# Softmax maxima over partitions: from a GpSimd all-reduce to VectorE's 32x32 transposes, with the subtraction on GpSimd

## The chip, the cores and the metric

One core of a Trainium2 chip. The time is device microseconds of one execution of the whole program. Five engines run their own queues in order: TensorE (PE), VectorE (DVE), ScalarE (ACT), GpSimd (POOL) and SyncE (SP, which issues most DMAs). Each engine does its instructions in the order of the program and waits on semaphores for what it needs.

## The reference

An attention block and a gated feed-forward block on the same input, mixed by a gate; all in float32. S = 2048 tokens, D = 448, 16 heads of 28, F = 1792.

```
g = sigmoid((x * gate_w).sum(-1))
q, k, v = heads of x @ wqkv
a = softmax(q k^T * 28**-0.5) v @ wo
b = (relu(x @ W_gate) * (x @ W_up)) @ W_down
out = g * a + (1 - g) * b
```

The softmax needs, for each query, a number near the maximum of its 2048 scores, to be subtracted before the exponential.

## The kernel before

**Stages.** Up to about 122 us x is projected to q, k and v (lines 292 to 510). Then come 32 *visits* of attention, two for each head: an even visit takes the first 1024 keys of a head, an odd one the other 1024. From about 1063 us the rest of the feed-forward block and the output projection run.

**Two ways to a maximum.** Scores are kept transposed, keys on partitions and queries along the free dimension. For 1536 of the 2048 queries of a head (three blocks of 512) the maximum is found ahead of time: `smax` (L161) computes the scores a second time with queries on partitions (products *sm*, L169), DVE reduces each of them with L171, and after the last one `smax_end` (L178) turns the maxima into two more rows of Q, so that the products *s* of the visit (L264, in `score`) come with the maximum already subtracted, and ACT applies the exponential straight from PSUM (L268). For the fourth block (`TQ = 1`) the raw scores are copied out by ACT with the sign turned (L270) into *quads*, tiles of 128 x 4 x 512. `block_min` takes the minimum over their chunks on DVE (L220, L222, into `r2`, then L228 into `rm`, L230 or L232 for the sign and the two halves); `all_max` reduces `rm` over the partitions on GpSimd (L238); `take_max` adds it to each of the two quads on DVE (L247); `take_exp` applies the exponential on ACT (L254). `rescale` brings the first half of a head to the maximum of the second (L592, L595, L596).

**The order.** It is written out by hand as strings, one per visit (L45 to L53), read letter by letter by the loop at L667: `s` a pair of score products, `m` an sm product with its L171, `x` one matmul of the feed-forward block (L554, filling PE's time), `b` a step of `block_min`, `A` is `all_max`, `g` is `take_max`, `e` is `take_exp`, `P` and `Q` the two halves of the product with V (`pv`, L608, after which L616 on DVE adds the two halves of a head), `w` the splitting of feed-forward weights (L109), `c` and `f` the two parts of `rescale`, `n` is `smax_end`. Visit 0 uses FIRST, visits 3, 8, 11 and 20 WIDE (called *long* here, four units of the feed-forward block), the other visits up to 28 LONG (*short*, three units), and 29 to 31 LATE, where no sm products are left. The minima of a visit are taken ahead of its `A`, at the end of the visit before.

**PSUM.** Every s and sm product takes one of three buffers of 128 x 1024 (`ps_w`, L92): two of tag `mx` and one of tag `w`, every third product the latter. An s is emptied by ACT, an sm by DVE's L171.

Of the kernel before, what the change touches and what calls it, by code (L numbers as in the profile page):

```python
# [1 line left out]

# [17 lines left out]
P = 128  # L20
# [9 lines left out]
TB = 512  # L30
# [36 lines left out]
def gated_mix_kernel(ctx, tc, x, wq, wo, wgu, wd, out):  # L67
    nc = tc.nc
# [30 lines left out]
    def ps_x(name):  # L99
        return psum.tile([P, TB], F32, tag="x", bufs=2, name=name)  # L100
# [89 lines left out]
    AT, QUAD, slots = {}, {}, iter(range(10 ** 6))  # L190
# [15 lines left out]

    stream = [p for v in range(2 * H) for p in visit(v)]
    todo_max, todo_sub, todo_exp, todo_all = [], [], [], []
    RM, R2, left = {}, {}, {}

    def block_min():

        if not todo_max:
# [13 lines left out]
        RM[v, b] = r  # L227
        nc.vector.tensor_tensor(r, r2[:, 0], r2[:, 1], op=OP.min)  # L228
        if v % 2:
            nc.vector.scalar_tensor_tensor(r, r, -1.0, RM[v - 1, b], op0=OP.mult, op1=OP.max)  # L230
        else:
            nc.vector.tensor_scalar(r, r, -1.0, None, op0=OP.mult)  # L232
        q = NK // 8 * (v % 2)
        todo_all.append((v, b, [(v, j, q), (v, j, q + 1)]))

    def all_max():
        v, b, quads = todo_all.pop(0)
        nc.gpsimd.partition_all_reduce(RM[v, b], RM[v, b], P, bass_isa.ReduceOp.max)  # L238
        todo_sub.extend((v, b, q) for q in quads)

    def take_max(way):
        v, b, q = todo_sub.pop(0)
        m = RM[v, b].unsqueeze(1).to_broadcast([P, 4, TB])
        if way == "d":
            nc.gpsimd.dma_start(QUAD[q], m, accum_op=OP.add)
        else:
            nc.vector.tensor_tensor(QUAD[q], QUAD[q], m, op=OP.add)  # L247
# [44 lines left out]
    with tc.tile_pool(name="qkv", bufs=1) as pa:  # L292
# [189 lines left out]
        m, first, ahead = 0, 9, NM[0] + NM[1] // 2  # L482
# [38 lines left out]
    att = stk.enter_context(tc.tile_pool(name="att", bufs=1))  # L521
# [395 lines left out]
```

## Time and profile before

| | us |
|---|---|
| median of 2 runs (1269.86 to 1271.8) | 1270.83 |
| the profiled execution | 1270.4 |
| its span | 1268.6 |
| PE busy | 1238.7 |
| DVE busy | 973.5 |
| ACT busy | 765.0 |
| POOL busy | 159.2 |

Engines overlap, so the busy times don't add up to the span. A busy PE is not a PE at its peak. The granted TensorE clock was 0.997 of full speed over the span. What counts is which engine's wait ends last at each place; the rows are read in the prediction. In rows of the timeline the columns are start, length, engine, line, operation, output<-input, shapes, count, and in brackets the idle time ahead with what ended it. In rows of groups: line, engine, operation, shapes, count, then busy us and mean ns of one, then idle us ahead. In rows of waits: who waited for whom, us in total, times, the longest.

### The profile page before, as it was taken

Reading aid. Unit: us, or ns where it says so; the run is one execution under the profiler, and the core shown is the slowest. Engines: PE = TensorE matmul, PEld = TensorE weight load, DVE = VectorE, ACT = ScalarE, POOL = GpSimd, SP = SyncE. Lnnn points to the kernel's source line nnn. Section 1 sums busy time; section 2 is a strip of 40 time slices with the busy share of each in tenths; the row PEclk is TensorE's granted clock in tenths of the full one; section 3 lists DMA queues with packets and bytes.
Section 4 is the critical chain, followed back from the end, with each engine's and each line's share of the span. In section 5 each row is a group of like instructions: output and inputs, shape, how many; then the busy total and the mean of one; then the engine's idle time right before and its main releaser. Section 6 shows DMA issues by size and latency. Waiting matters only on the chain.

```text
span 1268.6 us, 16622 instructions
## 1 busy us (share of the span) xinstructions
PE 1238.7 (98%) x6431; PEld 865.4 (68%) x6431; DVE 973.5 (77%) x985; ACT 765.0 (60%) x894; POOL 159.2 (13%) x146
## 2 busy tenths in 40 slices
PE   9999899999999999999999999999999799999998
PEld 6888556656566666666666666666666466899998
DVE  6466799999999989899998899898998262563342
ACT  5312667868676777777776767767766684222121
POOL 4222100000010000000001000000001011541020
PEclk9999999999999999999999999999999899999999
DMA  8946544352527252524545251424442226744432
GB/s 299 313 184 237 159 144 123 121 171 75 167 70 243 103 150 75 151 68 119 146 148 141 78 150 55 133 95 112 120 153 91 76 91 212 230 142 153 138 112 79
DMA packets 64299, 178.48 MB, mean 141 GB/s; under 512 B 13746, under 2 KB 20594, under 8 KB 59570
## 3 DMA queue, kind: packets, MB, share of 16 engines
q1 hardware_dynamic: 57484, 151.13, 39.5%
q0 software_dynamic: 6304, 25.82, 5.3%
q8 instruction: 51, 0.84, 0.3%
q10 hardware_dynamic: 432, 0.46, 0.1%
q14 instruction: 28, 0.23, 0.1%
HBM read 118.58 MB, written 58.87 MB: 140 GB/s over the span
## 4 chain that ended last, share of the span: by engine, by line
PE 86%; DVE 6%; ACT 3%; DMA 3%; issue 1%; POOL 1%; SPq 0%; ACTq 0%; DVEq 0%; POOLq 0%
PE gu L554 19%; PE s L264 18%; PE po L608 16%; PE sm L169 13%; PE acc L816 10%; PE qk L385 5%; PE wo L775 3%; PE v L403 3%; DVE mx L171 2%; ACT P L268 1%; DVE wg L109 1%; DVE P L247 1%; ACT P L254 1%; DVE r L222 1%; DMA wg<-ws_d 1%
## 5 line engine op out<-in xcount | busy, mean ns | idle before, releaser
L171 DVE TENSOR_REDUCE mx<-sm 128x1 f32<-128x1024 f32 x384 | 459.2, 1218 | 68.1 <-PE sm L169 66.7
L554 PE MATMUL gu<-X,wg 128*128 128x512 f32 x1232 | 366.8, 395 | 2.2 <-DMA wg<-ws_d 2.2
L268 ACT ACTIVATE P<-s 128x1024 f32<-128x1024 f32 x306 | 295.1, 1025 | 94.3 <-PE s L264 92.6
L264 PE MATMUL s<-Q,K 128*128 128x512 f32 x1024 | 318.3, 403 | 13.7 <-DMA Q<-mh 6.4
L554 PEld LDWEIGHTS gu<-X,wg 128*128 128x128 f32 x1232 | 231.3, 188 | 60.5 <-DMA wg<-ws_d 2.6
L169 PE MATMUL sm<-K,Q 128*128 128x512 f32 x768 | 242.5, 398 | 6.7 <-DVE mx L171 4.3
L264 PEld LDWEIGHTS s<-Q,K 128*128 128x128 f32 x1024 | 184.8, 189 | 85.8 <-issue 18.5
L608 PE MATMUL po<-P,V 128*32 128x512 f32 x1640 | 227.6, 596 | 0.8 <-ACT P L254 0.8
L169 PEld LDWEIGHTS sm<-K,Q 128*128 128x128 f32 x768 | 134.1, 188 | 55.7 <-DVE mx L171 13.2
L238 POOL PARTITION_ALL_REDUCE rm<-rm x32 | 66.5, 2079 | 832.2 <-DVE rm L230 415.3
L608 PEld LDWEIGHTS po<-P,V 128*32 128x32 f32 x1640 | 61.0, 110 | 119.4 <-issue 117.0
L816 PE MATMUL acc<-WD,hh 128*128 128x448 f32 x672 | 138.5, 365 | 0.0
L270 ACT ACTIVATE P<-s 128x1024 f32<-128x1024 f32 x104 | 105.9, 1026 | 52.9 <-PE s L264 50.3
L816 PEld LDWEIGHTS acc<-WD,hh 128*128 128x128 f32 x672 | 126.2, 188 | 10.4
L247 DVE TENSOR_TENSOR P<-P,rm 128x2048 f32<-128x2048 f32 x52 | 117.5, 2268 | 5.6 <-POOL rm L238 5.6
L608 PE MATMUL po<-V 128*32 128x512 f32 x408 | 116.4, 597 | 0.0
L103 ACT ACTIVATE hh<-hr 128x512 fp32r<-128x512 f32 x56 | 35.3, 631 | 118.7 <-PE acc L816 113.3
L254 ACT ACTIVATE P<-P 128x2048 f32<-128x2048 f32 x52 | 99.5, 1913 | 2.3 <-DVE P L247 2.1
L109 DVE TENSOR_TENSOR hh<-hr,hh 128x512 fp32r<-128x512 f32 x56 | 49.1, 877 | 62.4 <-ACT hh L103 62.4
L268 ACT ACTIVATE V<-s 128x1024 f32<-128x1024 f32 x78 | 76.3, 1026 | 22.1 <-PE s L264 21.6
L385 PE MATMUL qk<-X,W 128*128 128x512 f32 x308 | 77.4, 397 | 0.4 <-DVE X L109 0.2
L567 DVE TENSOR_TENSOR h<-gu,rl 128x512 f32<-128x512 f32 x56 | 38.2, 681 | 42.9 <-ACT rl L564 21.7
(82 smaller groups left out, 858.1 us busy)
## 6 DMA issues: line engine op xcount, KB each, us to landing
wg<-ws_d SPq DMA_DIRECT2D x42, 896.0 KB
K<-qk_d SPq DMA_DIRECT2D x64, 224.0 KB
Q<-qk_d SPq DMA_DIRECT2D x64, 224.0 KB
h_d<-h SPq DMA_DIRECT2D x56, 256.0 KB
hr<-h_d SPq DMA_DIRECT2D x56, 256.0 KB
ws_d<-wg SPq DMA_DIRECT2D x14, 896.0 KB
qk_d<-st POOLq DMA_DIRECT2D x21, 512.0 KB, 3.3
wgr<-wgu SPq DMA_DIRECT2D x13, 512.0 KB
```

Source lines behind the costliest of these rows:

```text
L169: nc.tensor.matmul(ps[:, c, :], Q[h][:, u * P:(u + 1) * P], K[h % 3][:, k0:k0 + TB], start=True, stop=True)
L171: nc.vector.tensor_reduce(MX[h][:, 2 * u + half:2 * u + half + 1], ps, axis=AX.XY, op=OP.max)
L238: nc.gpsimd.partition_all_reduce(RM[v, b], RM[v, b], P, bass_isa.ReduceOp.max)
L247: nc.vector.tensor_tensor(QUAD[q], QUAD[q], m, op=OP.add)
L254: nc.scalar.activation(q, q, AF.Exp, scale=-SCALE)
L264: nc.tensor.matmul(ps[:, c], K[h % 3][:, k * P:(k + 1) * P], Q[h][:, j * TB:(j + 1) * TB], start=True, stop=True)
L268: nc.scalar.activation(dst, ps, AF.Exp, scale=SCALE)
L270: nc.scalar.activation(dst, ps, AF.Copy, scale=-1.0)
L385: nc.tensor.matmul(ps, W[:, a, c * P:(c + 1) * P], xf(tb, b), start=(n == 0), stop=(n == NT - 1))
L554: nc.tensor.matmul(ps, WS[i][:, s, a], xf(i // NF, b), start=(n == 0), stop=(n == NT - 1))
L608: nc.tensor.matmul(po[32 * j:32 * j + 32], V[:, h // 4 % 2, k, h % 4], AT.pop((v, k, j)), start=(k == k0), stop=(k == k0 + NK // 2 - 1))
L816: nc.tensor.matmul(ACC[i // NF][t][:, :D], HH[i][:, a, t * P:(t + 1) * P], WD[:, f, b], start=(f == 0 and n == 0), stop=(f == NF - 1 and n ...
```

## The change

The maximum over partitions leaves GpSimd. `all_max` now does on DVE: a transposing reduction of `r2` (each 32 x 32 block is transposed and reduced over what were its 32 partitions), three copies that bring the other three groups of 32 partitions to the first, a reduction over the four groups and both halves of `r2` (and, in an odd visit, over the result of the even one), three copies back to the other groups, and a transpose of the repeated result that gives a tile of 128 x 512 with the same row on every partition. `take_max` subtracts it from the quads on GpSimd, a quarter of a quad at a time. L228, L230, L232 and the all-reduce go, and both `g` stand right behind `A`. `rescale` subtracts 32 x 16 numbers and transposes them.

```
-FIRST = "mmbslmxusbssmsxbxsxmxxsmxxmmsxxsxsAxgbxsmsbxxxxmmxegmxxbxxPweQ"
+FIRST = "mmbslmxusbssmsxbxsxmxxsmxxmmsxxsxsAggxbxsmsbxxxxmmxemxxbxxPweQ"
-LONG = "AnsmsxxxxsxxssxgmxxxxsmsxxsxssgxmxsxxmsmxxxmsmxxxxscmxsxemxxxbxxsmxbmbPefwQ"
+LONG = "AggnsmsxxxxsxxssxmxxxxsmsxxsxssxmxsxxmsmxxxmsmxxxxscmxsxemxxxbxxsmxbmbPefwQ"
...
-        r, r2 = att.tile([P, TB], F32, name=f"rm_{v}_{b}", tag=f"rm{v % 2}{b}", bufs=1), R2[v, b]
-        nc.vector.tensor_tensor(r, r2[:, 0], r2[:, 1], op=OP.min)
-        if v % 2:
-            nc.vector.scalar_tensor_tensor(r, r, -1.0, RM[v - 1, b], op0=OP.mult, op1=OP.max)
-        else:
-            nc.vector.tensor_scalar(r, r, -1.0, None, op0=OP.mult)
...
     def all_max():
-        nc.gpsimd.partition_all_reduce(RM[v, b], RM[v, b], P, bass_isa.ReduceOp.max)
+        v, b, j, quads = todo_all.pop(0)
+        h, odd = v // 2, v % 2
+        if not odd:
+            MN[h, b] = att.tile([P, 10, 16], F32, name=f"mn_{h}_{b}", tag=f"mn{b}", bufs=1)
+        n, to = MN[h, b], 8 + odd
+        nc.vector.tensor_reduce(n[:, :2], R2.pop((v, b)).rearrange("p a (b r) -> p a b r", r=32), axis=AX.X, op=OP.min,
+                                apply_transpose=True)
+        for k in range(1, 4):
+            nc.vector.tensor_copy(n[:32, 2 * k:2 * k + 2], n[32 * k:32 * k + 32, :2])
+        nc.vector.tensor_reduce(n[:32, to], n[:32, :to].rearrange("p a b -> p b a"), axis=AX.X, op=OP.min)
+        for k in range(1, 4):
+            nc.vector.tensor_copy(n[32 * k:32 * k + 32, to], n[:32, to])
+        RM[v, b] = att.tile([P, TB], F32, name=f"rm_{v}_{b}", tag="rm", bufs=2)
+        nc.vector.transpose(RM[v, b], n[:, to].unsqueeze(2).to_broadcast([P, 16, 32]))
         todo_sub.extend((v, b, q) for q in quads)
...
-            nc.vector.tensor_tensor(QUAD[q], QUAD[q], m, op=OP.add)
+        for c in range(0, 4, 1):
+            nc.gpsimd.tensor_tensor(QUAD[q][:, c], QUAD[q][:, c], RM[v, b], op=OP.subtract)
...
-        nc.gpsimd.partition_all_reduce(warm_r, warm_r, P, bass_isa.ReduceOp.max)
...
-                nc.vector.tensor_tensor(RS[h][r], RM[v - 1, b][r], RM[v, b][r], op=OP.subtract)
+                w = MN[h, b]
+                nc.vector.tensor_tensor(MN[h, 0][r, 0], w[r, 9], w[r, 8], op=OP.subtract)
+            nc.vector.transpose(RS[h][rows], MN[h, 0][rows, 0].unsqueeze(2).to_broadcast([32 * n, 16, 32]))
```

WIDE and LATE change in the same way: `gg` right behind `A`, and no other `g`. The orders of PE, ACT and SP stay as they are; those of DVE and POOL move. Where lines shift, the rows of the changed program carry its own line numbers (L170 is the old L171, L265 the old L264).

**DVE at the start of visit 16** (a short even visit; `r_16` is the `r2` of that visit, `mn` and `rm` the small tile and the result, `sm` the first sm product of the visit). Before:

```order
508 L222 TENSOR_TENSOR r_16_0_4973<-r_16_0_4973,P_3_1_4959 128x1024
509 L228 TENSOR_TENSOR rm_0_4998<-r_16_0_4973 128x512
510 L232 TENSOR_SCALAR rm_0_4998<-rm_0_4998 128x512
511 L596 TENSOR_TENSOR os_4803<-os_4803,rs_4952 32x512
512 L616 TENSOR_TENSOR os_4803<-po_5001,os_4803 128x512
513 L171 TENSOR_REDUCE mx_4825<-sm_5047 128x1
514 L247 TENSOR_TENSOR P_3_0_4932<-P_3_0_4932,rm_0_4998 128x2048
```

Now:

```order
531 L221 TENSOR_TENSOR r_16_0_5178<-r_16_0_5178,P_3_1_5164 128x1024
532 L596 TENSOR_TENSOR os_4992<-os_4992,rs_5156 32x512
533 L616 TENSOR_TENSOR os_4992<-po_5203,os_4992 128x512
534 L234 TENSOR_REDUCE mn_0_5243<-r_16_0_5178 128x32
535 L237 COPY mn_0_5243<-mn_0_5243 32x32 x3
536 L238 TENSOR_REDUCE mn_0_5243<-mn_0_5243 32x16
537 L240 COPY mn_0_5243<-mn_0_5243 32x16 x3
538 L242 STREAM_TRANSPOSE rm_0_5252<-mn_0_5243 128x512
539 L170 TENSOR_REDUCE mx_5031<-sm_5267 128x1
```

What stood ahead of L616 (L228, L232) is gone, and nine steps stand between L616 and the first reduction of the visit's sm products.

**DVE in visit 11** (a long odd visit, where `A` stands behind the second `m`). Before:

```order
393 L171 TENSOR_REDUCE mx_3888<-sm_3889 128x1
394 L171 TENSOR_REDUCE mx_3888<-sm_3904 128x1
395 L171 TENSOR_REDUCE mx_3888<-sm_3914 128x1
396 L247 TENSOR_TENSOR P_3_2_3751<-P_3_2_3751,rm_0_3818 128x2048
397 L247 TENSOR_TENSOR P_3_3_3776<-P_3_3_3776,rm_0_3818 128x2048
```

Now:

```order
407 L170 TENSOR_REDUCE mx_4025<-sm_4041 128x1
408 L234 TENSOR_REDUCE mn_0_3746<-r_11_0_3930 128x32
409 L237 COPY mn_0_3746<-mn_0_3746 32x32 x3
410 L238 TENSOR_REDUCE mn_0_3746<-mn_0_3746 32x16
411 L240 COPY mn_0_3746<-mn_0_3746 32x16 x3
412 L242 STREAM_TRANSPOSE rm_0_4054<-mn_0_3746 128x512
413 L170 TENSOR_REDUCE mx_4025<-sm_4068 128x1
```

The chain stands between the second and the third reduction, and the two L247 behind them are gone.

**PE in visit 16**, from its fourth product (`s_0_2`) on; in brackets the engines whose semaphores a row waits for. Before:

```order
2044 L264 MATMUL s_0_2_5061<-Q_1182,K_104 128x512 [waits Activation_49]
2045 L264 MATMUL s_0_2_5061<-Q_1182,K_104 128x512
2046 L554 MATMUL gu_0_5055<-X_111,wg_4869 128x512
2047 L554 MATMUL gu_0_5055<-X_112,wg_4869 128x512
2048 L264 MATMUL s_2_0_5068<-Q_1182,K_104 128x512 [waits DVE_49]
2049 L264 MATMUL s_2_0_5068<-Q_1182,K_104 128x512
2050 L264 MATMUL s_3_0_5072<-Q_1182,K_104 128x512 [waits Activation_49]
2051 L264 MATMUL s_3_0_5072<-Q_1182,K_104 128x512
2052 L554 MATMUL gu_0_5055<-X_111,wg_4869 128x512
2053 L169 MATMUL sm_5078<-K_102,Q_105 128x512 [waits Activation_49]
```

Now:

```order
2040 L265 MATMUL s_0_2_5281<-Q_1179,K_104 128x512 [waits Activation_49]
2041 L265 MATMUL s_0_2_5281<-Q_1179,K_104 128x512
2042 L552 MATMUL gu_0_5275<-X_111,wg_5074 128x512
2043 L552 MATMUL gu_0_5275<-X_112,wg_5074 128x512
2044 L265 MATMUL s_2_0_5288<-Q_1179,K_104 128x512 [waits Activation_49]
2045 L265 MATMUL s_2_0_5288<-Q_1179,K_104 128x512
2046 L265 MATMUL s_3_0_5292<-Q_1179,K_104 128x512 x2
2047 L552 MATMUL gu_0_5275<-X_111,wg_5074 128x512
2048 L168 MATMUL sm_5297<-K_102,Q_105 128x512 [waits DVE_49]
2049 L168 MATMUL sm_5297<-K_102,Q_105 128x512
```

PE's order is the same, but the wait for DVE, that is for the buffer of the visit's first sm product, has moved from the fifth product of the visit to the seventh, and the fifth waits for ACT. The buffers of the two are handed out when the program is built, by its own estimate of which comes free first. So it is in visits 4, 10, 16, 22 and 28; in 6, 12, 18 and 24 the wait for DVE stands at the eighth product, with the sixth waiting for ACT; in 2, 14 and 26 it stays at the fifth. In the long visits 8, 11 and 20 the buffer of the third sm product stays with the eleventh product, and in 3 it moves to the fourteenth.

More of the change, by code (lines that the diff above doesn't have):

```diff
@@ L3 @@
 import concourse.bass as bass
-import concourse.bass_isa as bass_isa
 import concourse.tile as tile
@@ L43 @@
 NP = 10
-FIRST = "mmbslmxusbssmsxbxsxmxxsmxxmmsxxsxsAxgbxsmsbxxxxmmxegmxxbxxPweQ"
-LONG = "AnsmsxxxxsxxssxgmxxxxsmsxxsxssgxmxsxxmsmxxxmsmxxxxscmxsxemxxxbxxsmxbmbPefwQ"
-WIDE = "ssnsxxmxxxsxxxmxAsmxxsxsxxxssxxxsxxgsxgmxxxsxmsxemxcxxxxmsxmxxxxxbsmbxxsxxmxxxemmbfPwQ"
-LATE = "xssxbxxxbxsAxsgxxgxsxxxsxxxsxxxsxsexxsxxwxsxxxxxxsxxxxcxxxsxxxxxxfnesbssPQ"
+FIRST = "mmbslmxusbssmsxbxsxmxxsmxxmmsxxsxsAggxbxsmsbxxxxmmxemxxbxxPweQ"
+LONG = "AggnsmsxxxxsxxssxmxxxxsmsxxsxssxmxsxxmsmxxxmsmxxxxscmxsxemxxxbxxsmxbmbPefwQ"
+WIDE = "ssnsxxmxxxsxxxmxAggsmxxsxsxxxssxxxsxxsxmxxxsxmsxemxcxxxxmsxmxxxxxbsmbxxsxxmxxxemmbfPwQ"
+LATE = "xssxbxxxbxsAggxsxxxsxxxsxxxsxxxsxsexxsxxwxsxxxxxxsxxxxcxxxsxxxxxxfnesbssPQ"
 ROUNDS = [(FIRST, 2)] + [(WIDE, 4) if k in (2, 7, 10, 19) else (LONG, 3) for k in range(2 * H - 4)] + [(LATE, 4)] * 3
@@ L208, in gated_mix_kernel @@
     todo_max, todo_sub, todo_exp, todo_all = [], [], [], []
-    RM, R2, left = {}, {}, {}
+    RM, R2, MN, left = {}, {}, {}, {}
     def block_min():
@@ L242, in take_max @@
         v, b, q = todo_sub.pop(0)
[L243 to L247, printed above, removed]
+        for c in range(0, 4, 1):
+            nc.gpsimd.tensor_tensor(QUAD[q][:, c], QUAD[q][:, c], RM[v, b], op=OP.subtract)
         todo_exp.append(q)
@@ L427, in gated_mix_kernel @@
         nc.vector.memset(warm, 0.0)
-        warm_r = pa.tile([P, 16], F32, name="warm_r")
-        nc.vector.memset(warm_r, 0.0)
         ps = ps_x("warm_ps")
```

4 lines of the change are left out of this document (1 added, 3 removed).

## Prediction

> **What bounds the kernel now.** I read the page's busy line first, then busy time by stretch, then PE's waits.
>
> ```profile
> PE 1238.7 (98%) x6431; PEld 865.4 (68%) x6431; DVE 973.5 (77%) x985; ACT 765.0 (60%) x894; POOL 159.2 (13%) x146
> 747.00:971.00 224.00, 224.00 (x1222) 142.69 (x1221) 202.85 (x191) 161.17 (x170) 17.25 (x12) 1.00 0.38 111
> PE s L264 <- DVE mx L171: 5.9, 9, 1.8
> PE sm L169 <- DVE mx L171: 4.3, 4, 2.1
> ```
>
> PE sets the end: in eight visits of attention (the second row: length, then PE, PEld, DVE, ACT, POOL) it is busy for all of 224 us, while DVE works 91% of them. Only 30 us of the span are without PE, so no relief of another engine can bring more, and what DVE costs PE is 5.9 + 4.3 = 10.2 us, none of it in that stretch. So the question is not how much DVE work goes, but whether DVE is late somewhere that PE stands waiting. Such a place exists at the start of every visit: each product (s or sm) takes one of three PSUM buffers, and PE needs a buffer back about three products later. A visit's first sm is given back by its L171.
>
> **What goes and what comes, on DVE.**
>
> ```profile
> L228 DVE TENSOR_TENSOR rm<-r 128x512 f32<-128x512 f32 x32 | 22.2, 692 | 1.1
> L232 DVE TENSOR_SCALAR rm<-rm 128x512 f32<-128x512 f32 x16 | 6.8, 427 | 0.5
> L247 DVE TENSOR_TENSOR P<-P,rm 128x2048 f32<-128x2048 f32 x52 | 117.5, 2268 | 5.6 <-POOL rm L238 5.6
> L171 DVE TENSOR_REDUCE mx<-sm 128x1 f32<-128x1024 f32 x384 | 459.2, 1218 | 68.1 <-PE sm L169 66.7
> L515 DVE TENSOR_SCALAR e<-e 128x16 f32<-128x16 f32 x1 | 0.2, 174 | 1.3 <-ACT e L514 1.3
> L109 DVE TENSOR_TENSOR mh<-mr,mh 16x128 fp32r<-16x128 f32 x16 | 4.4, 278 | 17.4 <-ACT mh L185 17.4
> ```
>
> Gone per visit: L228 0.69, L232 0.43 or its odd twin L230 at about 0.69, two L247 of 2.27: 5.8 us. New is one unbroken chain of nine steps. Nothing in the trace transposes, so I price by size. The transposing reduction of 1024 elements like L171, 1.22; six copies of 16 or 32 elements like L515, 0.18 each, 1.08; the reduction of 128 or 144 elements like mh, 0.29; the transpose to 512 elements like L228, 0.69; eight gaps of 0.03 (below, L232 starts 0.73 after an L228 of 0.69). Together **3.52 us**. Bounds: if the copies overlap and cost about half, and the second reduction 0.18, 2.5 us; if both transposing steps run at half rate (1.05 and 0.53 more), 5.1 us. I take 3.52, since each step has a row of its own size. L592 becomes a small step and a transpose, 0.17 longer, every other visit. DVE is thus relieved of about 2.2 us a visit, but the chain stands in one piece at the start of a visit, where before only L228 and L232 stood, ahead of PE's P and Q products.
>
> [...]
>
> **Start of a short even visit (v=16).**
>
> ```profile
> 609.50 0.69 DVE L228 TENSOR_TENSOR rm<-r 128x512 f32<-128x512 f32 x1
> 610.23 0.43 DVE L232 TENSOR_SCALAR rm<-rm 128x512 f32<-128x512 f32 x1
> 611.47 0.73 PE L264 MATMUL s<-Q,K 128*128 128x512 f32 x2
> 611.61 0.69 DVE L616 TENSOR_TENSOR os<-po,os 128x512 f32<-128x512 f32 x1 [0.24 <-PE po L608]
> 612.70 1.22 DVE L171 TENSOR_REDUCE mx<-sm 128x1 f32<-128x1024 f32 x1 [0.40 <-PE sm L169]
> 614.63 2.86 ACT L268 ACTIVATE P<-s 128x1024 f32<-128x1024 f32 x3 [0.39 <-PE s L264]
> 614.83 1.09 PE L264 MATMUL s<-Q,K 128*128 128x512 f32 x4
> 615.98 0.63 PE L169 MATMUL sm<-K,Q 128*128 128x512 f32 x2
> ```
>
> L616 waits for the last P and Q product and ends at 612.30 whatever goes before it. The chain stands behind it: 612.3 to 615.85. The first L171, done at 613.92 now, ends at 617.05. PE's fifth product, which takes that buffer today, starts at 614.83: **2.2 us** lost where the order stays so (v=14, 26; also 2). In other visits the buffers are handed out anew, as the order with the change shows. In v=10, 16, 22, 28 (and 4) the seventh product takes it; its fifth waits for ACT to empty the fourth (615.66), and the seventh, 615.98 today, for 617.05: **1.07**. In v=12, 18, 24 (and 6) it is the eighth; the sixth waits for ACT to empty the fifth, about 616.6 instead of 615.3: **1.3**. Sum of the nine from v=10: 2 x 2.2 + 4 x 1.07 + 3 x 1.3 = 12.6 us.
>
> **Odd visits (v=15)** have L634 in L616's place, and it waits for no product.
>
> ```profile
> 582.03 0.69 DVE L634 TENSOR_TENSOR os<-os,rb 128x512 f32<-128x512 f32 x1
> 584.50 0.28 DVE L109 TENSOR_TENSOR mh<-mr,mh 16x128 fp32r<-16x128 f32 x1 [1.79 <-ACT mh L185]
> 584.71 1.21 DVE L171 TENSOR_REDUCE mx<-sm 128x1 f32<-128x1024 f32 x1
> 586.62 0.63 PE L264 MATMUL s<-Q,K 128*128 128x512 f32 x2
> ```
>
> Without L228 and L230, L634 moves up 1.4 to 580.65, the chain runs 581.4 to 584.95, and mh and L171 end at 586.4, just ahead of 586.62: 0. The 1.79 us that DVE waits here today hide it; with a chain of 5.1 they would not, and nine visits would lose 1.4 each.
>
> **Long visits (v=11)** have the chain between the second and third L171.
>
> ```profile
> 472.96 2.38 DVE L171 TENSOR_REDUCE mx<-sm 128x1 f32<-128x1024 f32 x2 [0.35 <-PE sm L169]
> 473.46 0.62 PE L169 MATMUL sm<-K,Q 128*128 128x512 f32 x2
> 476.24 1.08 PE L264 MATMUL s<-Q,K 128*128 128x512 f32 x4
> ```
>
> The second ends at 474.15, the chain at 477.65, the third at 478.87. Its buffer is wanted at 476.24: 2.6 each in v=8, 11, 20; in v=3, where a later product takes it, I put ACT's 1.3. Sum 9.1.
>
> **Early visits**, with weight splits (L109) ahead of the chain:
>
> ```profile
> 265.23 1.19 PE L264 MATMUL s<-Q,K 128*128 128x512 f32 x4 [1.75 <-DVE mx L171]
> 353.28 1.21 DVE L171 TENSOR_REDUCE mx<-sm 128x1 f32<-128x1024 f32 x1
> ```
>
> Here DVE is already what PE waits for. Less 1.2 (L228, L232) and plus 3.55, the first L171 ends 2.35 later: v=2 loses 2.3; v=4, whose wait moves to the seventh product, 1.2; v=6, to the eighth, 0.2. In v=5 and 7 the L171 of the second row has 0.2 to spare and comes 2.1 later: 1.9 each. Sum 7.5.
>
> **GpSimd.** Eight subtractions of 512 elements a visit.
>
> ```profile
> L112 POOL TENSOR_TENSOR WD<-wdr,WD 128x448 fp32r<-128x448 f32 x14 | 21.4, 1527 | 51.5 <-DMA wdr<-wd 27.7 <-DVE WD L106 23.7
> L112 POOL TENSOR_TENSOR on<-or,on 128x1024 fp32r<-128x1024 f32 x8 | 19.6, 2456 | 56.2 <-ACT on L103 56.2
> 633.60 1.91 ACT L254 ACTIVATE P<-P 128x2048 f32<-128x2048 f32 x1
> ```
>
> Between the two sizes lie 1.61 ns an element, so 1.63 us a quarter, 6.5 a quad, 13.0 a visit: in v=16 from 615.85 to 628.9, ahead of the second exp (L254) at 633.60, which PE's delay moves back by another microsecond; the first exp needs only the quad that is ready at 622.4. Cost 0, as long as a quarter stays under (634.7 - 615.85) / 8 = 2.35 us. Beyond that ACT would stand at the exp, and behind it in ACT's queue the emptying of PSUM buffers that PE wants. Queued behind the quarters on GpSimd is only the small memset of m (L175), needed at the end of the visit: 0. The warm-up all-reduce at the program's start and its memset go too; only GpSimd's own memsets stood behind them: 0.
>
> [...]
>
> ```profile
> 155.52 2.28 DVE L247 TENSOR_TENSOR P<-P,rm 128x2048 f32<-128x2048 f32 x1
> 163.39 2.28 DVE L247 TENSOR_TENSOR P<-P,rm 128x2048 f32<-128x2048 f32 x1
> 165.70 1.91 ACT L254 ACTIVATE P<-P 128x2048 f32<-128x2048 f32 x1 [1.90 <-DVE P L247]
> 167.66 0.62 PE L608 MATMUL po<-P,V 128*32 128x512 f32 x1 [0.77 <-ACT P L254]
> 170.11 3.46 DVE L109 TENSOR_TENSOR wg<-wgr,wg 128x384 fp32r<-128x384 f32 x6
> 1085.33 0.39 DVE L106 CAST WD<-wdr 128x448 fp32r<-128x448 f32 x1
> 1093.99 4.44 POOL L112 TENSOR_TENSOR WO<-wor,WO 128x1344 fp32r<-128x1344 f32 x2 [6.66 <-DVE WO L106]
> 1094.12 3.28 DVE L106 CAST WD<-wdr 128x448 fp32r<-128x448 f32 x1
> 1099.87 0.69 DVE L567 TENSOR_TENSOR h<-gu,rl 128x512 f32<-128x512 f32 x1 [0.90 <-ACT rl L564]
> ```
>
> In v=0 the chain follows at once and P and Q come within 10 us. It starts at about 154.6 (L228, L232 gone), ends at 158.1; eight quarters end at 171.1, the second exp at 173.0, against 167.6 now: 5.4 us that PE waits. Moreover the last four rows show the two engines in each other's way: a cast of 0.39 us took 3.28 beside a subtraction on GpSimd, while L567, with one input from PSUM, was not held. In v=0 three two-input minima (L220 and L222, 1024 elements, so 1.22 like L171) and six splits (3.46) fall among the quarters: up to 7.1 more, 12.5 in all. Downward, up to 2.1 us that PE waits for L171 today (the longest of the four waits above) can vanish with the L247s: 3.3. I take 7, nearer the row without locking, because DVE has long waits of its own there; bounds 3 and 12. [...]
>
> The last visits:
>
> ```profile
> 1042.73 4.49 DVE L247 TENSOR_TENSOR P<-P,rm 128x2048 f32<-128x2048 f32 x2 [1.98 <-POOL rm L238]
> ```
>
> There are no maxima there. Before, L228, L230, this row's wait of 1.98 and one L247 are 5.6 us to the first quad; now the chain and four quarters are 10.1. Most of these 4.5 us lie beside scores that ACT empties anyway; I put 1.5 for v=30 and 31 together, bounds 0 and 4.
>
> **Sum.** 12.6 + 9.1 + 7.5 + 7 + 1.5 = 37.7; ACT catches up while PE stands, which saves small waits, 3 by guess. 34.7 on the profiled execution's 1270.4 (span 1268.6, 0.4 below the median of 1270.83) gives **1305 us**.
>
> **Rivals.** (1) The relief wins, the other side: if the chain takes under 1.3 us (fifth product) or 2.5 (seventh), L171 gives its buffer back in time, nothing is lost, and some 8 of the 10.2 us that PE waits for DVE go: 1262. For it: DVE loses 2.2 us a visit; against: nine dependent steps. Chance 0.07. (2) A chain of 2.5 with little locking: 4 x 0.9 + 3 x 1.3 + 2 x 1.2, long visits 6.1, early 3.9, v=0 3, less 3, is 20: 1290. Chance 0.19. (3) Half-rate transposes, 5.1: even 22, odd 13, long 14, early 15, ends 11, less 3: 1342. Chance 0.10. (4) GpSimd quarters of 2.7 us, held by DVE: the second exp is 2.8 late in 28 visits, 78 more: 1383. Against it: in that window DVE mostly runs L171, which reads PSUM, as the unheld L567 does. Chance 0.05. The forecast keeps 0.59.
>
> **Numbers.** Range 1286 to 1332: it leaves out (1), (3) and (4) in part. A measurement of this kernel tells about 2% (25 us) from no change. Slower by more than that: 0.70 (nearly all of the forecast, (3), (4)); within it 0.28 ((1), (2), the forecast's low edge); faster 0.02, as PE has but 30 us free.
>
> **What would show it.** Right: a chain near 3.5 us behind L616; PE standing 1 to 2.6 us for L171 or ACT early in even and long visits, not in odd ones from v=9; short visits of 28.2 us (fifth product to fifth product, 586.62 to 614.83) becoming about 29.6 where they are even; quarters of 1.6 us; P of v=0 split by a wait of 5 us or more; DVE busy some 70 us less (32 x 2.2). Wrong: no new waits of PE on L171, a chain under 2.5 or over 4.5, or L171 longer than 1.22 beside GpSimd.

## The result, and the profile after

The changed kernel takes **1312.65 us** (median of 1310.53 and 1314.77) against 1270.83: a ratio of 1.033, 95% interval 1.025 to 1.041. That is 42 us slower; 1305 was forecast. The profiled execution took 1314.77 us, its span is 1313.0, 44.4 more than before; all readings below are against that span.

The busy line of the changed kernel's page, and PE's rows of its waits (who waited for whom, us in total, times, longest):

```profile
PE 1259.3 (96%) x6431; PEld 871.7 (66%) x6431; DVE 900.4 (69%) x1160; ACT 767.9 (58%) x894; POOL 416.9 (32%) x369
```

```profile
PE s L265 <- DVE mx L170: 16.2, 12, 2.5
PE s L265 <- ACT P L269: 8.4, 10, 1.2
PE sm L168 <- DVE mx L170: 6.1, 4, 3.3
PE po L608 <- ACT P L255: 3.6, 2, 3.0
```

Busy time by stretch, over the eight visits that the prediction shows (stretch, length, then PE, PEld, DVE, ACT and POOL busy, granted clock, DMA share, GB/s):

```profile
779.50:1012.30 232.80, 228.24 (x1221) 142.67 (x1221) 184.47 (x234) 161.87 (x170) 80.60 (x68) 0.99 0.35 105
```

DVE does 73 us less and PE waits for it more: 22.3 us instead of 10.2, and 8.4 for ACT's emptying of s products instead of 1.1. PE's idle time, span less busy, went from 29.9 to 53.7 us. But PE's busy time grew too, by 20.6 us, with the same 6431 matmuls. The eight visits show both: 8.8 us longer, 4.2 of it with PE busy.

The chain in visit 16, in DVE's timeline (start, length), and PE's wait beside it:

```profile
637.37 0.69 DVE L616 TENSOR_TENSOR os<-po,os 128x512 f32<-128x512 f32 x1 [1.23 <-PE po L608]
637.98 1.23 DVE L234 TRANSPOSE_TENSOR_REDUCE mn<-r 128x32 f32<-128x1024 f32 x1
639.24 0.54 DVE L237 COPY mn<-mn 32x32 f32<-32x32 f32 x3
639.82 0.36 DVE L238 TENSOR_REDUCE mn<-mn 32x16 f32<-32x128 f32 x1
640.21 0.53 DVE L240 COPY mn<-mn 32x16 f32<-32x16 f32 x3
640.84 0.71 DVE L242 STREAM_TRANSPOSE rm<-mn 128x512 f32<-128x512 f32 x1
641.48 1.19 DVE L170 TENSOR_REDUCE mx<-sm 128x1 f32<-128x1024 f32 x1
641.43 1.19 PE L265 MATMUL s<-Q,K 128*128 128x512 f32 x4 [0.70 <-ACT P L269]
642.72 0.73 PE L168 MATMUL sm<-K,Q 128*128 128x512 f32 x2
```

From 637.98 to 641.55 is 3.57 us, nearly the 3.52 forecast, in one piece behind L616, which itself waits 1.23 us for PE. The first L170 stands behind it and ends at 642.67. PE stands twice here: 0.70 us at its fifth product, until ACT has emptied the fourth, and a little more at the seventh, the sm product at 642.72, which takes the buffer that this L170 gives back.

In the long visit 11 the chain stands ahead of the third L170, and PE's timeline shows what a longer wait brings:

```profile
493.34 0.86 PE L552 MATMUL gu<-X,wg 128*128 128x512 f32 x3
496.68 1.65 PE L265 MATMUL s<-Q,K 128*128 128x512 f32 x4 [2.47 <-DVE mx L170]
498.12 1.48 PE L552 MATMUL gu<-X,wg 128*128 128x512 f32 x3
501.35 0.39 PE L552 MATMUL gu<-X,wg 128*128 128x512 f32 x1
```

Busy time by stretch behind that wait:

```profile
496.70:500.10 3.40, 3.40 (x9) 2.71 (x10) 0.00 (x0) 1.94 (x2) 3.40 (x4) 0.57 0.00 0
```

After 2.47 us of waiting three matmuls of the same kind take 1.48 instead of 0.86 us: the granted clock is 0.57 in this stretch, and full again from 500.62 on. The visit loses 4.3 us, not 2.5. The mean granted clock of the span fell from 0.997 to 0.984, which is worth 21.0 - 3.8 = 17 us of full speed, part of it under the waits themselves. In the stretches at half speed PE was busy for 37.1 us, against 5.3 before; by estimate half of the difference, 16 us, is time that full speed would have saved (in the half-speed stretch of visit 11 one matmul follows another after 0.43 us, behind it after 0.23). So of the 44.4 us, 24 are more waiting and about 16 are PE at half speed behind waits. The last 5 are more busy time at full speed; a part of them is that the first matmuls behind a wait are shown some 0.1 us longer (0.73 for the pair at 642.72, 0.62 or 0.63 for pairs without a wait).

### The profile page after: what moved, and what is told of

Same layout as the page of the kernel before. It is cut to its first block, busy times and chain, and to the rows that moved or that the text cites. A ratio compares the mean times of both kernels' runs of the same rounds, so it can differ in the third digit from the quotient of the medians.

```text
span 1313.0 us, 17150 instructions
## 1 busy us (share of the span) xinstructions
PE 1259.3 (96%) x6431; PEld 871.7 (66%) x6431; DVE 900.4 (69%) x1160; ACT 767.9 (58%) x894; POOL 416.9 (32%) x369
## 4 chain that ended last, share of the span: by engine, by line
PE 83%; DVE 8%; ACT 3%; DMA 2%; issue 2%; POOL 2%; SPq 0%; DVEq 0%; ACTq 0%; POOLq 0%
PE gu L552 18%; PE s L265 17%; PE po L608 15%; PE sm L168 13%; PE acc L816 10%; PE qk L386 5%; DVE mx L170 3%; PE wo L775 3%; PE v L404 3%; ACT P L269 1%; POOL P L248 1%; DVE mn L234 1%; DVE r L221 1%; DMA wg<-ws_d 1%; DVE wg L108 0%
## 5 line engine op out<-in xcount | busy, mean ns | idle before, releaser
L170 DVE TENSOR_REDUCE mx<-sm 128x1 f32<-128x1024 f32 x384 | 459.1, 1217 | 169.6 <-PE sm L168 168.1
L248 POOL TENSOR_TENSOR P<-P,rm 128x512 f32<-128x512 f32 x208 | 265.0, 1313 | 508.3 <-DVE rm L242 468.9
L552 PE MATMUL gu<-X,wg 128*128 128x512 f32 x1232 | 374.0, 402 | 2.6 <-DMA wg<-ws_d 2.6
L265 PE MATMUL s<-Q,K 128*128 128x512 f32 x1024 | 325.1, 409 | 33.6 <-DVE mx L170 16.2
L552 PEld LDWEIGHTS gu<-X,wg 128*128 128x128 f32 x1232 | 236.4, 192 | 62.7 <-DMA wg<-ws_d 3.0
L265 PEld LDWEIGHTS s<-Q,K 128*128 128x128 f32 x1024 | 185.9, 191 | 113.4 <-DVE mx L170 26.4
L168 PE MATMUL sm<-K,Q 128*128 128x512 f32 x768 | 245.6, 402 | 7.5 <-DVE mx L170 6.1
L608 PE MATMUL po<-P,V 128*32 128x512 f32 x1640 | 230.7, 599 | 3.6 <-ACT P L255 3.6
L255 ACT ACTIVATE P<-P 128x2048 f32<-128x2048 f32 x52 | 99.5, 1913 | 12.9 <-POOL P L248 10.2
L248 POOL TENSOR_TENSOR V<-V,rm 128x512 f32<-128x512 f32 x48 | 60.6, 1295 | 118.3 <-DVE rm L242 73.7
```

The lines of the kernel that those rows point to most:

```text
L168: nc.tensor.matmul(ps[:, c, :], Q[h][:, u * P:(u + 1) * P], K[h % 3][:, k0:k0 + TB], start=True, stop=True)
L170: nc.vector.tensor_reduce(MX[h][:, 2 * u + half:2 * u + half + 1], ps, axis=AX.XY, op=OP.max)
L248: nc.gpsimd.tensor_tensor(QUAD[q][:, c], QUAD[q][:, c], RM[v, b], op=OP.subtract)
L255: nc.scalar.activation(q, q, AF.Exp, scale=-SCALE)
L265: nc.tensor.matmul(ps[:, c], K[h % 3][:, k * P:(k + 1) * P], Q[h][:, j * TB:(j + 1) * TB], start=True, stop=True)
L552: nc.tensor.matmul(ps, WS[i][:, s, a], xf(i // NF, b), start=(n == 0), stop=(n == NT - 1))
```

## The experiments

Where a visit's *lag* is told, it is the difference of the ends of its last P and Q product between two traces. All ratios are to the kernel before on the same chip.

**e1_early_chain.**

```
         todo_all.append((v, b, j, [(v, j, q), (v, j, q + 1)]))
+        all_max()
...
             elif o == "A":
-                all_max()
+                continue
```

> The chain of all_max is put directly behind the last minimum of a visit, at the end of the visit before, where the kernel before had L228 and L232; letter A does nothing. The chain's length, its nine steps and GpSimd's quarters stay. Theory 1 (the place of the chain costs: PE stands for a PSUM buffer early in even and long visits): these waits go; what stays is visit 0 (about 7 us) and a little of the early and last visits, so 1270.8 + 7 + 1 to 3 = about 1276 to 1282. Rival 2 (the mere amount of DVE work beside GpSimd, the two locking each other): stays at 1308 to 1316. Rival 3 (the subtraction on GpSimd comes too late for the exps): also stays, above 1305.

Measured: 1362.19 us, ratio 1.072 (1.069 to 1.075). Worse by 50 us than the change: theory 1, as far as "early is free" goes, fell. The start of visit 3 (POOL, DVE and PE in the timeline):

```profile
250.04 5.98 POOL L249 TENSOR_TENSOR P<-P,rm 128x512 f32<-128x512 f32 x4 [24.16 <-issue]
249.83 8.01 DVE L108 TENSOR_TENSOR wg<-wgr,wg 128x384 fp32r<-128x384 f32 x6
257.87 1.64 DVE L635 TENSOR_TENSOR os<-os,rb 128x512 f32<-128x512 f32 x1
259.43 1.34 DVE L108 TENSOR_TENSOR mh<-mr,mh 16x128 fp32r<-16x128 f32 x1
261.95 1.22 PE L266 MATMUL s<-Q,K 128*128 128x512 f32 x2 [7.89 <-DVE mx L170]
```

GpSimd starts as soon as rm is there, and now that is when DVE splits weights. The six splits take 8.01 us (3.46 before), L635 1.64 (0.69), mh 1.34 (0.28): the two engines hold each other up here. GpSimd's quarters take 1.5 us here, 1.3 elsewhere. So the change's late chain also kept the quarters beside the L170s, which read PSUM and stay at 1.22 there (1.19 to 1.23 for the 156 of them that fall beside quarters). The eight visits from 1 to 8 lost 65 us, with waits for DVE of up to 7.89 us. Half speed behind such waits is about 26 us of e1's whole loss: PE was busy for 57.9 us in such stretches, against 5.3 before.

**e2_gpsimd_sub** and **e3_dve_chain_sub**, each one half of the change.

```
 def take_max (e2: the all-reduce of before, strings of the change)
-            nc.vector.tensor_tensor(QUAD[q], QUAD[q], m, op=OP.add)
+        for c in range(0, 4, 1):
+            nc.gpsimd.tensor_tensor(QUAD[q][:, c], QUAD[q][:, c], RM[v, b], op=OP.add)
 def take_max (e3: the chain of the change, strings of before)
-            nc.gpsimd.tensor_tensor(QUAD[q][:, c], QUAD[q][:, c], RM[v, b], op=OP.subtract)
+        nc.vector.tensor_tensor(QUAD[q], QUAD[q], RM[v, b].unsqueeze(1).to_broadcast([P, 4, TB]), op=OP.subtract)
```

> Half of the change: the maximum as in the kernel before (L228, L230, L232 on DVE and the all-reduce on GpSimd), but the subtraction by GpSimd in quarters right behind A. Theory 1 (the chain's place costs): only visit 0 loses (second exp later by about two microseconds more than in the change, since the all-reduce stands ahead of the quarters), 7 to 9 us, while DVE is relieved of 4.5 us a visit; 1272 to 1281. Rival 3 (lateness of the subtraction on GpSimd costs): most of the 42 us are here too, 1300 or more. A switch of GpSimd between the all-reduce and elementwise work, if it costs microseconds, would show as gaps on GpSimd and a later exp in each visit.

> The other half: the chain on DVE right at A as in the change, but the subtraction on DVE, a whole quad at a time, at the places where the kernel before has it. Theory 1: the waits of even and long visits stay (about 25 us with the half-speed clock behind them in the long ones), visit 0 loses only the longer chain, 1 to 3 us; with DVE 2.3 us a visit busier than before, 1300 to 1312. Rival 3 (GpSimd's subtraction costs): 1271 to 1280.

e2: 1307.07 us, 1.027 (1.025 to 1.030). e3: 1313.3, 1.032 (1.030 to 1.034). e3 loses as much as the change with nothing of the subtraction on GpSimd, as theory 1 had it. That the two are equal is chance: its visit 0 lost 3.2 us instead of 7.2, and its nine even visits from 10 on 20.0 instead of 14.8, seven of them with a second wait of 0.3 to 0.7 us, probably by the L247s that stand behind the chain. e2 lies where rival 3 had it, not where theory 1 had it. It is no clean counter-test, because of a cost that only this mixture has (POOL in the timeline of e2):

```profile
622.30 2.25 POOL L238 PARTITION_ALL_REDUCE rm<-rm  x1 [8.94 <-DVE rm L232]
633.78 6.31 POOL L244 TENSOR_TENSOR P<-P,rm 128x512 f32<-128x512 f32 x5 [9.24 <-issue]
```

Between the all-reduce and the first quarter GpSimd stands 7 to 10 us without waiting for anything shown (239 us in 32 visits). Neither kernel pays that in attention, where each gives GpSimd only one of the two. The last three visits lost 18.6 of e2's 37.7 us, visit 0 6.7, with waits of PE for ACT of up to 7.0 us there; what the other 12 are stays open. So e2 does not tell whether the change's own subtraction comes too late; e3 does, whose even and long visits wait without it.

e3 also separates the clock from the wait. Its long visits 8, 11 and 20 wait the same, and only the first is followed by half speed (PE's timeline):

```profile
403.60 2.07 PE L264 MATMUL s<-Q,K 128*128 128x512 f32 x4 [2.37 <-DVE mx L170]
496.84 1.21 PE L264 MATMUL s<-Q,K 128*128 128x512 f32 x4 [2.40 <-DVE mx L170]
765.65 1.19 PE L264 MATMUL s<-Q,K 128*128 128x512 f32 x4 [2.37 <-DVE mx L170]
```

From just ahead of the wait to 4.5 us behind it PE falls 4.0, 2.7 and 2.6 us further behind the kernel before: half speed costs 1.3. In the change, with half speed in all three, it falls 4.3, 4.3 and 4.2. (Over the whole of visit 8 both get back 1.3 us at two places where the kernel before waited.)

**e4_short_chain** leaves out the copies and the combination over the groups, **e7_long_chain** does the last step three times.

```
-        for k in range(1, 4): ... (both loops of copies, e4)
-        nc.vector.tensor_reduce(n[:32, to], n[:32, :to].rearrange("p a b -> p b a"), axis=AX.X, op=OP.min)
+        nc.vector.tensor_reduce(n[:, to], n[:, :2].rearrange("p a b -> p b a"), axis=AX.X, op=OP.min)
 e7:
+        for _ in range(3):
             nc.vector.transpose(RM[v, b], n[:, to].unsqueeze(2).to_broadcast([P, 16, 32]))
```

> The change without the six small copies and the reduction over the groups: each group of 32 partitions subtracts its own minimum of one half (the combination of the four groups and the two halves is left out). Chain 1.24 + about 0.3 + 0.71 = 2.25 us instead of 3.5, at the same place. The wait in long visits becomes 1.2 instead of 2.47, those in even visits lose up to 1.27. If only the waits count: 3 long, 9 even, about 5 early and visit 0 save about 21 us, 1292. If a wait of 2 us or more also brings a window of 3.4 us at half the granted clock (costing 1.7 us of work), those windows go as well (some 9 of them, 15 us): about 1278. The visits 8, 11 and 20 tell it apart: 1.3 us shorter each by the first, 3 us by the second.

> The change with the last step of the chain (the transpose to 128 x 512, 0.71 us) done three times, so a chain of 4.9 us at the same place. Waits only: 9 even visits, 3 long ones and some 5 early ones lose 1.42 us more each, ten odd visits lose the 1.2 us for which their slack does not suffice: about 37 us, 1350. If a PE wait of 2 us or more brings a window at half the granted clock, the even visits (waits of 0.7 to 1.2 us in the change, now 2.1 to 2.6) join the long ones: seven windows of 1.7 us more, about 1362, and the record of the granted clock shows a half-speed window at nearly each even visit.

e4: 1286.09 us, 1.012 (1.010 to 1.014), between the two estimates. Its long visits lose 0.1, 1.9 and 1.4 us instead of 2.9, 4.3 and 4.2: 2.4 to 2.8 less for a chain 1.3 shorter, near the 3 us of the second estimate. Between visits 1 and 28 no half-speed stretch is left, and the longest wait of an s product for an L170 is 1.1, as its waits show:

```profile
PE s L261 <- DVE mx L170: 8.5, 16, 1.1
```

e7: 1347.06, 1.060 (1.057 to 1.062), as the waits alone had it; a half-speed window in nearly each even visit did not come. The reason is in PE's timeline:

```profile
601.02 2.08 PE L266 MATMUL s<-Q,K 128*128 128x512 f32 x4 [3.48 <-DVE mx L170]
662.05 1.19 PE L266 MATMUL s<-Q,K 128*128 128x512 f32 x4 [0.70 <-ACT P L270]
511.32 2.08 PE L266 MATMUL s<-Q,K 128*128 128x512 f32 x4 [3.97 <-DVE mx L170]
```

Where the build hands the buffers out anew (the second row, visit 16), no wait of the even visits from 10 on is over 1.2 us, though the chain is 4.9 us long; in visits 10, 16, 22 and 28 PE stands the same 0.70 us for ACT with a chain of 2.3 (e4), 3.6 and 4.9 us. There the hand-out of the buffers sets the wait more than the chain's length does. Where the order stays (visit 14, the first row, and the long visits, the third), the wait grows with the chain. Half speed follows in those, but not in visit 26, behind a wait of 3.49 us.

**e8_early_chain_dve_sub** is e1 with e3's subtraction; **e9_split_chain** puts all of the chain but the transpose (L242) behind the last minimum and leaves the transpose at A; **e10_split_chain_v0** adds visit 0's subtraction on DVE.

```
 e9:  todo_all.append((v, b, [(v, j, q), (v, j, q + 1)]))
+        group_max(v, b)        # L234 to L240
 e10: take_max
+        if v == 0:
+            nc.vector.tensor_tensor(QUAD[q], QUAD[q], RM[v, b].unsqueeze(1).to_broadcast([P, 4, TB]), op=OP.subtract)
```

> The chain at the end of the visit before, as in e1_early_chain, but the subtraction on DVE at the places of the kernel before: nothing of the maximum is left on GpSimd. In e1_early_chain GpSimd's quarters began at once and fell on the weight splits (L108 x6 8.01 us instead of 3.46), which is taken here for the cause of its loss. If so, this is 1272 to 1284 (2.4 us a visit more DVE work than before, at a place with cover). If instead the chain at the end of a visit is itself what costs (DVE late there whatever GpSimd does), it stays above 1300, nearer the 1362 of e1_early_chain.

> The chain in two: everything up to the copies back (2.8 us) at the end of the visit before, only the transpose to 128 x 512 (0.71 us, where the kernel before had L228 and L232 of 1.1) at A; GpSimd's quarters therefore start at A as in the change, beside maxima that read PSUM and not beside the weight splits. Theory 1 with locking: even visits 0, long ones under 0.7, visit 0 about 5 us, last visits 1.5, less some of the 10 us that PE waited for DVE before: 1268 to 1280. If the mere presence of GpSimd's quarters costs (rival 2) or the length of the chain wherever it stands, 1300 or more.

> e9_split_chain, and in visit 0 alone the subtraction on DVE, a whole quad at a time, at the places of the kernel before. Visit 0 is where P and Q follow the subtraction within 10 us and where GpSimd's quarters fall on weight splits. Theory: 4 to 6 us less than e9_split_chain, 1263 to 1274, level with the kernel before or up to 0.5% faster. If the price of visit 0 in the change (7.2 us) came from the chain and not from GpSimd, no difference from e9_split_chain.

e8: 1299.77 us, 1.023 (1.021 to 1.024): without the quarters e1's 91 us shrink to 28, although the subtraction is back on DVE. So the quarters in that place cost 62, half speed behind the waits included; but 28 is more than twice the most that was expected, 13 of it in visits 1 to 8. e9: 1294.53, 1.019 (1.017 to 1.021), above its forecast; its long visits lose nothing (0.0 to 0.4), as forecast, but each short even visit 0.5 to 1.1. DVE and PE at the start of its visit 16:

```profile
627.44 0.69 DVE L620 TENSOR_TENSOR os<-po,os 128x512 f32<-128x512 f32 x1
628.04 0.70 DVE L246 STREAM_TRANSPOSE rm<-mn 128x512 f32<-128x512 f32 x1
628.67 1.19 DVE L170 TENSOR_REDUCE mx<-sm 128x1 f32<-128x1024 f32 x1
629.91 1.19 PE L269 MATMUL s<-Q,K 128*128 128x512 f32 x4 [0.81 <-DVE mx L170]
```

The last product L620 needs is out, and L620 no longer waits for PE (1.23 us in the change): DVE has no slack there for 2.8 us more, whoever subtracts. e10: 1293.36, 1.018 (1.015 to 1.020): no difference from e9 in time, where 4 to 6 us less were expected. Visit 0 ends 4.0 behind instead of 6.6, and visit 1 loses another 1.8.

**e6_v0_on_dve** does the same to the change itself (the edit is e10's).

> The change with the subtraction of visit 0 alone on DVE, a whole quad at a time, at the places of the kernel before; the chain stays where it is. The prediction's term for visit 0 was 7 us (7.2 measured at the end of that visit) and was put down to the quarters on GpSimd. If that holds, the chain's own 2.3 us of delay is all that is left: visit 0 ends about 2.5 to 3.5 us behind the kernel before and the whole is 1306 to 1310. If the term came from the chain on DVE, nothing changes (7 us, 1312).

1310.06 us, 1.029 (1.027 to 1.032), at the upper edge. Visit 0 ends 2.5 behind instead of 7.2, as expected, but visit 1 loses another 3.3. DVE in visit 0, and PE in visits 0 and 1:

```profile
158.01 2.29 DVE L248 TENSOR_TENSOR P<-P,rm 128x2048 f32<-128x2048 f32 x1
162.62 1.22 PE L168 MATMUL sm<-K,Q 128*128 128x512 f32 x2 [5.70 <-DVE mx L170]
179.08 1.88 PE L267 MATMUL s<-Q,K 128*128 128x512 f32 x4 [1.83 <-DVE mx L170]
```

The subtraction now stands with the chain ahead of an L170, and PE waits 5.70 us for it there instead of 3.34. Visit 1's loss is another thing: its own chain (174.18 to 177.73) stands ahead of its first L170, and PE waits 1.83 us and goes on at half speed. In the change PE came 4.7 us later to this place and did not have to wait.

**e11_chain_behind_first_sm** moves letters only; **e12_chain_behind_v0** adds visit 0.

```
-LONG = "Aggnsmsxxxxsxxssxmxxxxsmsxxsxssxmxsxxmsm...
+LONG = "nsmAggsxxxxsxxssxmxxxxsmsxxsxssxmxsxxmsm...
-WIDE = "ssnsxxmxxxsxxxmxAggsmxxsxsxxxss...
+WIDE = "ssnsxxmxxxsxxxmxsmAggxxsxsxxxss...
 e12, with e10's edit in take_max:
-FIRST = "...sxmxxsmxxmmsxxsxsAggxbxsmsbxxxxmmxemxxbxxPweQ"
+FIRST = "...sxmxxsmxxmmsAxxsxsxgbxsmsbxxxxmmxegmxxbxxPweQ"
```

> The change with 'Agg' moved by a few letters and nothing else: in short visits behind the first m (its L170 then stands ahead of the chain), in long ones behind the third m. e9_split_chain still lost about 1.0 us in each even visit because DVE has no slack at the end of a visit; here the chain falls where the kernel before had the first L247 (2.3 us), with DVE idle behind it. PE's products take the same PSUM buffers as in the kernel before. Theory 1 (the first L170s behind the chain are the whole loss of even and long visits): 0 in even and long visits, no half-speed windows there; visit 0 keeps its 7 us, early and last visits 1 to 4: 1274 to 1283. Rival 2 (chain plus GpSimd's quarters cost wherever they stand): above 1290.

> As e11_chain_behind_first_sm, and visit 0 with its subtraction on DVE (a whole quad at a time, at the places of the kernel before) and its chain a little earlier, behind the ninth s, where DVE stood idle. In e10_split_chain_v0 visit 0 lost 4.0 us with DVE's subtraction against 6.7 with GpSimd's in e9_split_chain, but the next visit gave most of it back. Theory: visit 0 loses 2 to 4 us instead of 7: 1270 to 1279, 3 to 5 us under e11_chain_behind_first_sm. If visit 1 gives it back again: no difference.

e11: 1291.05 us, 1.015 (1.014 to 1.017): 22 us for a few letters, and no half-speed window between visit 1 and the last ones. But it is above the forecast and just where rival 2 had it, so its time does not tell the two apart. Its visits do: from 10 on the short even ones lose 0.3 to 0.4 and the long ones 0.6 and 0.0, where the change lost 1.1 to 3.8 and 4.2 to 4.3. The short odd ones lose 0.6 to 0.9, so a part of the delay has moved there, and visit 0 still loses 7.6. e12: 1282.94, 1.009 (1.008 to 1.011), 8 us less than e11 by its visit 0, yet above its forecast too. It is 1.4 us ahead of the kernel before after visit 8; then every short visit loses about 0.4 (even) or 0.7 (odd). In visit 15 of e12 PE now waits for the second L170 (DVE, PE):

```profile
590.58 0.71 DVE L242 STREAM_TRANSPOSE rm<-mn 128x512 f32<-128x512 f32 x1
591.21 1.19 DVE L170 TENSOR_REDUCE mx<-sm 128x1 f32<-128x1024 f32 x1
592.45 0.73 PE L267 MATMUL s<-Q,K 128*128 128x512 f32 x2 [0.40 <-DVE mx L170]
```

**e13_split_behind_l170** fits the chain into the holes that the removed work left.

```
 block_min, behind the last minimum: L234 alone (the transposing reduction)
 all_max: the rest
+ODD = "AggnsmsxxxxsxxssxmxxxxsmsxxsxssxmxsxxmsmxxxmsmxxxxscmxsxemxxxbxxsmxbmbPefwQ"
+ROUNDS: WIDE in visits 3, 8, 11, 20, ODD in the other odd ones from 7 on, e12's LONG elsewhere up to 28
+        if v == 0 or v > 28:   # on DVE, v > 28 at the places of the kernel before
```

> From e12_chain_behind_v0, whose short visits from v=9 on still lost 0.4 (even) to 0.7 us (odd) each, while it was 1.4 us ahead of the kernel before after v=8. The first step of the chain (the transposing reduction, 1.24 us) goes to the end of the visit before, in place of L228 and L232 (1.1); the rest (2.25 us) stands in even visits behind the first m, in place of the first L247 (2.28), in odd visits from v=7 on at the front, ahead of mh, where DVE stood idle for 3.3 us. The last three visits subtract on DVE at the places of the kernel before. If the loss is only a matter of which L170 stands behind how many us of DVE work, each visit from v=9 on now costs 0, and the whole stands at 1268 to 1274, level with the kernel before. If GpSimd's quarters or the chain have another price, it stays at 1280 or above.

1272.4 us, ratio 1.0016 (1.0005 to 1.0027) in eleven runs: within 0.3% of the kernel before, not faster, and 40 us under the change. Its page's busy line, and DVE in the timeline of visit 16:

```profile
PE 1240.1 (98%) x6431; PEld 865.0 (68%) x6431; DVE 919.5 (72%) x1168; ACT 765.6 (60%) x894; POOL 373.5 (29%) x337
```

```profile
608.89 1.25 DVE L233 TRANSPOSE_TENSOR_REDUCE mn<-r 128x32 f32<-128x1024 f32 x1
610.96 0.69 DVE L621 TENSOR_TENSOR os<-po,os 128x512 f32<-128x512 f32 x1
611.84 1.22 DVE L172 TENSOR_REDUCE mx<-sm 128x1 f32<-128x1024 f32 x1 [0.19 <-PE sm L170]
613.10 0.54 DVE L240 COPY mn<-mn 32x32 f32<-32x32 f32 x3
614.70 0.71 DVE L245 STREAM_TRANSPOSE rm<-mn 128x512 f32<-128x512 f32 x1
615.78 1.22 DVE L172 TENSOR_REDUCE mx<-sm 128x1 f32<-128x1024 f32 x1 [0.37 <-PE sm L170]
```

1.25 us stand where L228 and L232 had 1.1, the other 2.3 where an L247 had 2.3, and both L172 wait for PE as before. With the same transposes, the quarters of 28 of 32 visits on GpSimd and 54 us less DVE work than before, next to nothing is lost and nothing gained. So the loss was a matter of place, not of the amount of work: that of the chain, and in visit 0 and the last visits that of the subtraction. The short visits from 9 on now cost 0, as forecast, but for 9, 21, 23, 25 and 27, which lose 0.5 to 0.7 each. The last three lose 0.4 or more in every version, e2 without a chain among them; why stays open. No version beat the kernel before.

## Where the prediction was right, and where not

**Right: the mechanism.** The chain took 3.57 us for 3.52, each step within 0.1 us of its row of like size; the quarters 1.31 where 1.63 was taken (first row of GpSimd's groups: count, busy us, mean ns), which lay off the path outside visit 0, where PE's only two waits for L255 are; DVE is busy 73 us less for 70. Seventh-product visits lost 1.1 (forecast 1.07), eighth-product ones 1.4 to 1.5 (1.3). Odd visits from 9 on lost 0 to 0.2 (0), but 23, 25 and 27 lost 0.4 each. e3 shows such waits with nothing of the subtraction on GpSimd, e11 to e13 that the chain's place decides. One bound was worked out too low: copies at half price and a second reduction of 0.18 make the short chain of the second rival 2.9 us, or 2.6 without the gaps, not 2.5.

```profile
L248 POOL TENSOR_TENSOR P<-P,rm 128x512 f32<-128x512 f32 x208 | 265.0, 1313 | 508.3 <-DVE rm L242 468.9 <-ACT P L269 39.4
```

**Right in size, partly by luck: visit 0**, 7.2 us for 7. GpSimd, ACT and PE in the changed kernel's timeline:

```profile
157.90 13.45 POOL L248 TENSOR_TENSOR P<-P,rm 128x512 f32<-128x512 f32 x8 [14.66 <-DVE rm L242]
171.38 1.91 ACT L255 ACTIVATE P<-P 128x2048 f32<-128x2048 f32 x1 [2.43 <-POOL m L174]
173.34 1.06 PE L608 MATMUL po<-P,V 128*32 128x512 f32 x1 [2.97 <-ACT P L255]
```

The path is the one forecast: the quarters end at 171.35 (forecast 171.1), and PE resumes at 173.34 (173.0), 5.7 us late. But the quarters came to that end by two errors that cancel. Beside L170s alone they took 1.28 us, not 1.63; beside DVE's two-input work (L219, L221, the splits) 1.6 to 2.3, where the forecast's 171.1 had no locking at all. And what came on top of the wait, 1.6 us put down to locking, was 1.5 us of half speed behind it. The six splits did take 6.01 us instead of 3.46; the minima beside the quarters kept 1.2, and there GpSimd was the one that was held. e6 adds what the forecast did not say: without this delay visit 1 loses 3.3 us by its own chain and the half speed behind it.

**Mis-sized: the long visits.** 2.6 us each were forecast, 2.9, 4.3 and 4.2 came, and with visit 3 13.0 in place of 9.1. The step that failed is not the wait, 2.47 of the 2.6, but the assumption that PE goes on at full speed after it. Two of the fifth-product visits show the price: behind the same wait of 2.00 us visit 14 lost 2.2, as forecast, and visit 26, with half speed, 3.8. Together the nine even visits from 10 on lost 14.8 for 12.6.

**Missing: the granted clock.** No term of the sum was for it, though the kernel before shows it once, half speed for 6.83 us around a wait of 6.40 in visit 29. It also lies in the 1.9 us that the part behind the last visit lost, where 0 was forecast. The length of the gap alone does not tell where it comes: a half-speed window followed gaps of 2.00 and of 2.37 to 2.47 us, and did not follow gaps of 2.37 and 2.40 in e3 and one of 3.49 in e7.

**Too high: the early visits** (2, 4, 5, 6, 7), 4.8 us for 7.5: visit 6 gained 2.1 where 0.2 was to be lost, 5 and 7 lost 1.2 each for 1.9, while 2 and 4 lost 3.2 and 1.4 (2.3 and 1.2), with half-speed windows. The last visits lost 1.1 for 1.5. Of the 3 us that ACT was to catch up, some came: three waits for ACT of the kernel before, 1.7 us in visits 6 and 8, are gone.

So the sum of 34.7 came near 44.4 without its largest missing term. Eight half-speed windows that nothing hid, at the 1.5 us of visit 26 each, are about 12 us by estimate; terms set too high covered a part of them. Of the rivals the second (a short chain) and third (half-rate transposes) fell with the chain's rows, the fourth with the quarters' 1.31 us. The first, that the relief wins, fell with PE's waits, and e13, the best place found, did not win either: PE had 29.9 us idle before, and 28.5 with 54 us less DVE work.

## What to carry to other kernels

Where one engine is busy nearly all the time, price an edit on another engine by what stands queued behind it there, and look for the hole that the removed work leaves: the same nine instructions went with a loss of 42 us in one place and of about 2 in the places of e13, which also moved the subtraction of four visits. Moving them earlier is no cure by itself: what they release then starts earlier too, and may meet other work (e1, another 50 us). Count what a stall brings behind it too: in the change, waits of PE of 2.46 and 2.47 us in visits 8, 11 and 20 and one of 2.00 in visit 26 were followed by 3.41 us at half the granted clock, worth another 1.3 to 1.5 us here.

## What was not expected of the hardware

- The half-speed stretches are 3.41 us long or a whole multiple of it (6.83), but for the one at the program's end, and in every trace their starts lie whole multiples of 3.41 us apart (in the change 4, 16, 35, 72 and so on behind the first, at 159.29). What tells the waits apart is how long PE stands within one stretch of that grid. Busy time by stretch on that grid, in the change, for visit 14 (the first two rows) and visit 26 (the last two), both with a wait of 2.00 us:

```profile
582.54:585.95 3.41, 1.97 (x9) 1.61 (x10) 1.42 (x3) 1.30 (x3) 2.99 (x3) 1.00 0.00 0
585.95:589.36 3.41, 3.41 (x16) 2.67 (x15) 2.57 (x3) 3.25 (x5) 3.41 (x4) 1.00 0.00 0
934.11:937.53 3.42, 1.48 (x7) 0.86 (x5) 3.19 (x9) 1.75 (x2) 0.96 (x1) 1.00 0.02 2
937.53:940.94 3.41, 3.35 (x8) 2.67 (x9) 0.01 (x1) 1.94 (x2) 3.41 (x4) 0.50 0.00 0
```

  Visit 14's wait falls on two stretches, with PE idle for at most 1.44 us of one; visit 26's falls in one, with 1.94, and half speed follows. So it is in all fourteen traces from 140 us on: of the stretches at full speed all 75 with PE idle for 1.9 us or more were followed by half speed, none of the 4525 with under 1.8, and one of the four between. (In the traces of the two kernels alone, the 13 with 1.9 us or more were all followed by it, and none of the 646 with at most 1.57.) Two short waits did it together in visit 4 of the change: 0.70 and 1.55 us left PE idle for 1.98 of one stretch. It settles e3 too (1.96 us in one stretch in visit 8, at most 1.49 and 1.72 in 11 and 20), and e7's wait of 3.49, cut into 1.82 and 1.67.
- GpSimd stood 7 to 10 us between an all-reduce and the first quarter of the subtraction (e2, 239 us in 32 visits).
- A tiny DVE instruction suffered from a neighbour as a large one did: mh, 16 x 128, took 1.34 us beside a quarter on GpSimd instead of 0.28 (e1). The change's L170s beside quarters, with their one input in PSUM, stayed at 1.22.
